# Window attention and two MLPs on one core: ScalarE's work for coming heads and GpSimd's low part of g put behind other instructions

## The chip, the core and the metric

The kernel runs on one core of one Trainium2 chip. The core has five engines that run side by side, each with a queue that it works through in order: TensorE (PE, with the weight load, PEld, shown apart), VectorE (DVE), ScalarE (ACT), GpSimd (POOL) and SyncE (SP), which issues the DMAs. The metric is the device time of one execution in microseconds (us), the median of three runs.

## The reference

Attention of 4 sequences of 576 tokens with 8 heads of 64 over a window of 128 tokens, with a slope per head, then two MLPs (512 to 2048 to 512) one after the other over all 2304 tokens.

```python
scores = scale * np.matmul(q, k.transpose(0, 1, 3, 2))
bias = slopes[:, None, None] * (-np.abs(rel).astype(np.float32))[None, :, :]
mask = (rel >= 0) & (rel < window)
scores = np.where(mask, scores + bias[None], -1000000000.0)
attn = np.exp(scores - np.max(scores, axis=-1, keepdims=True))
attn = attn / (np.sum(attn, axis=-1, keepdims=True) + 1e-09)
x = np.matmul(attn, v)           # to (tokens, heads * 64)
# first MLP
h = x @ w_in
g = np.where(h >= 1, h, np.where(h <= -1, 0.0, (h + 1) ** 2 / 4.0))
x = g @ w_out
# second MLP: h = x @ w_in2; g = h * clip(h + 3, 0, 6) / 6; out = g @ w_out2
```

## The kernel before

The tokens are cut into units of 64 to 256 queries. Each unit has 8 heads, so head 40 is the first of unit 5. A head's queries go in blocks of up to 128: heads 40 to 47, 56 to 63 and 88 to 95 have one block each, the other heads from 32 on have two. A step is one block of one head. Units 0 to 3 (heads 0 to 31) multiply in float32; from head 32 on every operand is split into a rounded high part and a low part (float32r), and only these heads' code is touched here.

The first MLP runs at the same time. It goes over blocks of tokens and 16 chunks f of its 2048 hidden columns. `Chunks.run` writes a chunk: 12 matmuls L659 into the bank h, then `between()`, in which an attention step (`tick`) may stand, then `flush`, the 12 matmuls L701 of the chunk two before (LAG = 2), then `after()`, where another step may stand. `activate` turns h into g: L688 on DVE, L689 on ACT, L690 on DVE, which frees the bank h, then g's high part on ACT (L152) and its low part on POOL (L159). From the wide blocks on there is one h bank, so that the next chunk's L659 waits for L690.

A step of a head from 32 on, `stage_a`: two matmuls L411 give the scores s from qs with kh and with kl. DVE masks and adds the slope (L438, L441, the smallest value by row), ACT takes exp with its sum (L445), DVE makes the reciprocal (L448, L449), POOL normalises p (L450). Three steps later, `stage_b`: PE transposes p (L470), ACT rounds the high part of it (L152, into tt, or into dist where a block has keys of the block before), DVE makes the low part (L483), and POOL cuts the two triangles (L488). Two steps after that, `stage_c`: L554 multiplies with vs into r. After a head's last block ACT and DVE add the halves of r to xf (L572), and after an odd head `to_x` casts xf to x, the MLP's input (L152 on ACT, L159 on DVE).

`prep(n)` casts a head's operands ahead: on ACT kh (L389) and the high part of qs (L390), on DVE kl (L391), on POOL the low part of qs (L393, with a memset L395 where a block is short), and for an even head vs (L152, L159). `tick` calls it right behind `stage_a` of a head's first block: for head n+1 where the heads have two blocks, and up to head n+2 where they have one.

```python
with self.behind():
    for x in late:
        self.to_x(*x)
    if i == 0:
        self.more_preps(n + 1 if u.whole or len(u.qbs) > 1 else n + 2)
```

The order within an engine is found by a scheduler while the program is built; SP's is as written. `tc.issue_after(ins)` binds it: what is written inside, on the engine of `ins`, stands behind `ins`. `behind()` opens it for the last L441 (`row`), L483 (`low`) and L572 (`sum`), all three on DVE. It holds for the casts and for `flush`.

Of the kernel before, what the change touches and what calls it, by code (L numbers as in the profile page):

```python
# [40 lines left out]
def tile_window_attention_two_mlps(  # L41
# [108 lines left out]
    def split_hi(eng, hi, x):  # L150
        if eng == "act":
            nc.scalar.copy(hi, x)  # L152
        elif eng == "pool":
            nc.gpsimd.tensor_scalar(out=hi, in0=x, scalar1=1.0, scalar2=1.0, op0=ALU.mult, op1=ALU.mult)
        else:
            engines[eng].tensor_copy(hi, x)

    def split_lo(eng, lo, x, hi):
        engines[eng].tensor_tensor(out=lo, in0=x, in1=hi.bitcast(F32), op=ALU.subtract)  # L159
# [110 lines left out]
    class Attention:  # L270
        def __init__(self, raw, proc, work, xs):
            self.raw, self.proc, self.work, self.xs = raw, proc, work, xs
            self.n_load = self.n_prep = self.t = 0
            self.row, self.low, self.sum, self.late = None, None, None, []
            self.k_owners, self.v_owners = [], []
# [138 lines left out]
        def stage_a(self, n, i):  # L414
# [20 lines left out]
            if not u.whole and a >= P:  # L435
# [8 lines left out]
                scalar=3.0e38, op0=ALU.add, op1=ALU.min, accum_out=sm[:, 0:1])  # L444
            nc.scalar.activation(out=pt[:, :nk], in_=pt[:, :nk], func=AF.Exp, bias=sm[:, 0:1],  # L445
                                 scale=-1.0, accum_out=None if u.whole else sm[:, 1:2])
            if not u.whole:
# [6 lines left out]
        def stage_b(self, n, i):  # L454
# [26 lines left out]
            hi, lo = both[:, 0], both[:, 1]  # L481
            split_hi(HI["th"], hi, src)
            self.low = nc.vector.tensor_tensor(out=lo, in0=src, in1=hi.bitcast(F32), op=ALU.subtract)  # L483
            if has_prev:


                for s, sign in ((0, -1), (1, 1)):
                    nc.gpsimd.affine_select(out=u.tt[:, :, s0 + s, :m], in_=both, compare_op=ALU.is_ge, fill=0.0,  # L488
                                            base=-1 + s, pattern=[[0, 2], [sign, m]], channel_multiplier=-sign)
# [140 lines left out]
        def behind(self):  # L630


            stack = ExitStack()
            for op in (self.row, self.low, self.sum):
                if op:
                    stack.enter_context(tc.issue_after(op.ins))
            return stack


    class Mlp:  # L640
        tags = ("h0", "h1")
        g_lo = "g"
# [29 lines left out]
    class Mlp1(Mlp):  # L672
        acc_tags = ("acc0", "acc1", "h1", "t2")
        lag = LAG

        def accs(self, n):
# [7 lines left out]
        def activate(self, ps, n):  # L684


            r, g = self.tiles()
            nc.vector.tensor_scalar(out=r[:, :n], in0=ps[:, :n], scalar1=-1.0, scalar2=1.0, op0=ALU.max, op1=ALU.min)  # L688
            self.square = nc.scalar.activation(out=r[:, :n], in_=r[:, :n], func=AF.Square, bias=0.5, scale=0.5)  # L689
            self.larger = nc.vector.tensor_tensor(out=r[:, :n], in0=ps[:, :n], in1=r[:, :n], op=ALU.max)  # L690
            split_hi(HI["g"], g[:, 0, :n], r[:, :n])
            split_lo(LO[self.g_lo], g[:, 1, :n], r[:, :n], g[:, 0, :n])
            return g
# [35 lines left out]
    class Mlp2(Mlp):  # L729
# [4 lines left out]
        def between(self):  # L734
            pass
# [43 lines left out]
    class Chunks:  # L779
# [22 lines left out]
        def run(self, mlp, blk, f, part, x, between, after, behind=ExitStack):  # L802
            self.pend.append((mlp, blk, f, part, mlp.first(x, f, mlp.blocks[blk][1])))
            between()
            with behind():
                self.flush(mlp.lag)
            after()
# [28 lines left out]
    def run_block(mlp1, j, part, hook):  # L836
        for f in part:
            chunks.run(mlp1, j, f, part, j, lambda: hook(f, 0), lambda: hook(f, 1), att.behind)

    with ExitStack() as actx:  # L840
# [507 lines left out]
```

## Time and profile before

| | us |
|---|---|
| median of 3 runs (lowest, highest) | 946.19 (946.13, 946.76) |
| profiled execution | 946.02 |
| its span, first to last instruction | 944.3 |
| TensorE busy in it | 928.5 (98%) |
| VectorE, ScalarE, GpSimd busy | 659.4, 535.6, 306.8 |

The split heads' attention and the first MLP run between about 165 and 480 us. The second MLP follows and is not touched. The granted TensorE clock is 1.000 of full speed over the span. A row of the timeline gives the start, the duration, the engine, the line and the operation as out<-in; consecutive instructions of one line stand in one row with their count (x12), and what is in brackets at its end is the engine's idle time before it and the instruction that ended it.

### The profile page before, as it was taken

How to read it: one execution, taken by the hardware profiler on the slowest of the kernel's cores; microseconds unless marked ns; L12 is line 12 of the kernel's file. 1: busy time of each engine (PE TensorE's matmuls, PEld its weight loads, DVE VectorE, ACT ScalarE, POOL GpSimd, SP SyncE). 2: the span in 40 equal slices, each digit the busy share in tenths (PEclk: the TensorE clock that was granted, in tenths of full speed). 3: DMA queues.
4: the chain of work that ended last, by engine and by line, in shares of the span. 5: the costliest groups of instructions: out<-in, count | busy, mean ns of one | idle time of the engine just before them, and what ended most of it. 6: DMA issues, size and time to landing. Idle time of an engine off the chain costs nothing.

```text
span 944.3 us, 17237 instructions
## 1 busy us (share of the span) xinstructions
PE 928.5 (98%) x5683; PEld 875.5 (93%) x5683; DVE 659.4 (70%) x1750; ACT 535.6 (57%) x1349; POOL 306.8 (32%) x575
## 2 busy tenths in 40 slices
PE   8899999999999999999999999999999999999998
PEld 6799999999999999999999999999999888898987
DVE  6998975786677677767656899958557777644443
ACT  6998854676667566666635786535333334423233
POOL 3243845787668676777710000000000000000000
PEclk9999999999999999999999999999999999999999
DMA  8858322232222212322017771004264654543431
GB/s 256 240 178 264 111 89 88 68 86 67 73 64 72 79 46 62 89 75 62 1 55 270 266 237 55 1 23 167 81 210 170 232 174 146 169 124 114 123 112 67
DMA packets 95337, 114.90 MB, mean 122 GB/s; under 512 B 8848, under 2 KB 73616, under 8 KB 95248
## 3 DMA queue, kind: packets, MB, share of 16 engines
q1 hardware_dynamic: 95248, 113.80, 38.3%
q8 instruction: 45, 0.74, 0.3%
q14 instruction: 44, 0.36, 0.1%
HBM read 88.60 MB, written 25.17 MB: 120 GB/s over the span
## 4 chain that ended last, share of the span: by engine, by line
PE 89%; DVE 5%; ACT 2%; DMA 2%; issue 1%; POOL 1%; SPq 0%; ACTq 0%; DVEq 0%; POOLq 0%
PE h L659 26%; PE acc L760 21%; PE acc L701 18%; PE y L1249 7%; PE x L1249 5%; PE s L411 4%; PE r L554 3%; PE t L470 2%; PE r L506 2%; DMA rawa<-w_in 1%; DVE r L688 1%; DVE kl L391 1%; DVE r L690 1%; DVE x L159 1%; DMA kw<-kT 1%
## 5 line engine op out<-in xcount | busy, mean ns | idle before, releaser
L659 PE MATMUL h<-x,wa 128*128 128x384 f32 (+1 forms) x1344 | 231.0, 317 | 1.4 <-DVE r L690 0.9
L701 PE MATMUL acc<-g,wa 128*128 128x384 f32 (+1 forms) x1344 | 227.4, 315 | 0.4 <-POOL g L159 0.4
L760 PE MATMUL acc<-wb,g 128*128 128x512 f32 x861 | 222.2, 393 | 0.0
L659 PEld LDWEIGHTS h<-x,wa 128*128 128x128 f32 x1344 | 206.8, 189 | 4.3 <-DVE r L690 3.4
L701 PEld LDWEIGHTS acc<-g,wa 128*128 128x128 f32 x1344 | 206.3, 189 | 0.7 <-POOL g L159 0.6
L760 PEld LDWEIGHTS acc<-wb,g 128*128 128x128 f32 x861 | 159.4, 188 | 24.9
L152 ACT CAST g<-r 128x384 fp32r<-128x384 f32 (+1 forms) x208 | 101.6, 489 | 71.4 <-DVE r L1196 37.6
L159 POOL TENSOR_TENSOR g<-r,g 128x256 fp32r<-128x256 f32 (+1 forms) x96 | 92.5, 964 | 67.7 <-ACT g L152 54.8
L689 ACT ACTIVATE r<-r 128x384 f32<-128x384 f32 (+1 forms) x112 | 53.5, 479 | 81.3 <-DVE r L688 81.0
L159 DVE TENSOR_TENSOR g<-r,g 128x384 fp32r<-128x384 f32 x112 | 62.4, 557 | 41.9 <-ACT g L152 41.6
L688 DVE TENSOR_SCALAR r<-h 128x384 f32<-128x384 f32 (+1 forms) x112 | 55.4, 495 | 44.0 <-PE h L659 37.3
L488 POOL TENSOR_SCALAR_AFFINE_SELECT tt<-dist 128x256 fp32r<-128x256 f32 (+1 forms) x176 | 76.9, 458 | 13.9 <-DVE dist L483 13.8
L690 DVE TENSOR_TENSOR r<-h,r 128x384 f32<-128x384 f32 (+1 forms) x112 | 55.8, 499 | 30.3 <-ACT r L689 28.4
L659 PE MATMUL h<-x,wb 128*128 128x384 f32 x384 | 72.5, 336 | 0.0
L659 PEld LDWEIGHTS h<-x,wb 128*128 128x128 f32 x384 | 68.2, 188 | 2.6
L445 ACT ACTIVATE p<-p,sm 128x128 f32<-128x128 f32 (+2 forms) x134 | 57.3, 430 | 20.9 <-DVE sm L441 20.5
L1194 ACT ACTIVATE r<-u 128x384 f32<-128x384 f32 x32 | 16.9, 527 | 56.2 <-DVE u L1258 56.2
L554 PEld LDWEIGHTS r<-tt,vs 128*128 128x128 f32 x304 | 44.7, 189 | 3.2 <-issue 1.4
L393 POOL TENSOR_TENSOR qs<-qr,qs 128x256 fp32r<-128x256 f32 (+2 forms) x64 | 39.4, 616 | 24.9 <-ACT qs L390 13.3
L554 PE MATMUL r<-tt,vs 128*128 128x128 f32 (+3 forms) x304 | 44.3, 262 | 1.4 <-POOL tt L488 0.9
L470 PE MATMUL t<-ident,p 128*128 128x128 f32 x134 | 38.4, 288 | 0.5 <-ACT tt L152 0.5
L1249 PE MATMUL y<-wb,w 128*128 128x384 f32 x192 | 38.7, 336 | 0.0
(161 smaller groups left out, 1554.6 us busy)
## 6 DMA issues: line engine op xcount, KB each, us to landing
w<-wd SPq DMA_DIRECT2D x88, 256.0 KB, 2.7
rawa<-w_in SPq DMA_DIRECT2D x16, 512.0 KB, 5.3
rawa<-w_out SPq DMA_DIRECT2D x16, 512.0 KB, 5.4
rawb<-w_in SPq DMA_DIRECT2D x16, 512.0 KB, 3.8
rawb<-w_out SPq DMA_DIRECT2D x16, 512.0 KB, 4.7
wd<-sum SPq DMA_DIRECT2D x32, 256.0 KB, 2.1
wd<-wb SPq DMA_DIRECT2D x24, 256.0 KB, 2.8
out<-o SPq DMA_DIRECT2D x17, 256.0 KB, 2.3
```

Source lines behind the costliest of these rows:

```text
L152: nc.scalar.copy(hi, x)
L159: engines[eng].tensor_tensor(out=lo, in0=x, in1=hi.bitcast(F32), op=ALU.subtract)
L445: nc.scalar.activation(out=pt[:, :nk], in_=pt[:, :nk], func=AF.Exp, bias=sm[:, 0:1], scale=-1.0, accum_out=None if u.whole else sm[:, 1:2])
L470: nc.tensor.transpose(ps[:, 1, :], pt[:, P:] if u.whole and has_prev else pt[:, :P], ident)
L488: nc.gpsimd.affine_select(out=u.tt[:, :, s0 + s, :m], in_=both, compare_op=ALU.is_ge, fill=0.0, base=-1 + s, pattern=[[0, 2], [sign, m]], ...
L554: nc.tensor.matmul(u.r[:, qo:qo + nq], u.vs[:, j, c, :, :].rearrange("p a d -> p (a d)"), u.tt[:, part].rearrange("p s q -> p (s q)")[:, s ...
L659: nc.tensor.matmul(ps[:, :n], self.W.w_in(a, c, f), self.x_chunk(x, b, c, n), start=(k == 0), stop=(k == 3 * KC - 1))
L688: nc.vector.tensor_scalar(out=r[:, :n], in0=ps[:, :n], scalar1=-1.0, scalar2=1.0, op0=ALU.max, op1=ALU.min)
L690: self.larger = nc.vector.tensor_tensor(out=r[:, :n], in0=ps[:, :n], in1=r[:, :n], op=ALU.max)
L701: nc.tensor.matmul(acc[i][:, o * n:(o + 1) * n], self.W.w_out(a, f)[:, e * P:(e + 1) * P], g[:, b, :n], start=(first and k == 0 and o == 0 ...
L760: nc.tensor.matmul(acc[t][:, :DM], g[:, b, tg * P:(tg + 1) * P], self.W.w_out(a, f), start=(first and k == 0), stop=(last and k == 2))
L1249: nc.tensor.matmul(ps[:, :N2], w[:, a, c * P:(c + 1) * P], self.x.operand(k, c, b), start=(start and n == 0), stop=(n == 5), skip_group_ch ...
```

## The change

`behind()` binds two more instructions: the last exp (L445) and the last rounded transpose (L152 in `stage_b`) of the heads from 32 on. Both are on ACT, so ACT's part of `prep`, of `to_x` and of `flush` stands behind them. The low part of g is no longer written in `activate` but in `Chunks.run`, after `between()`, and stands behind the last triangle (L488) on POOL. This holds in the blocks that `run_block` writes, once there has been a triangle. Computation and instruction counts stay the same.

```diff
--- before.py
+++ after.py
@@ -149,7 +149,7 @@
 
     def split_hi(eng, hi, x):
         if eng == "act":
-            nc.scalar.copy(hi, x)
+            return nc.scalar.copy(hi, x)
         elif eng == "pool":
             nc.gpsimd.tensor_scalar(out=hi, in0=x, scalar1=1.0, scalar2=1.0, op0=ALU.mult, op1=ALU.mult)
         else:
@@ -271,7 +271,7 @@
         def __init__(self, raw, proc, work, xs):
             self.raw, self.proc, self.work, self.xs = raw, proc, work, xs
             self.n_load = self.n_prep = self.t = 0
-            self.row, self.low, self.sum, self.late = None, None, None, []
+            self.row, self.low, self.sum, self.exp, self.high, self.tri, self.late = None, None, None, None, None, None, []
             self.k_owners, self.v_owners = [], []
 
             self.vts = [raw.tile([P, KCH, 2 * D + 2], F32, tag="vr", name=f"vr{i}", bufs=3) for i in range(3)]
@@ -442,8 +442,10 @@
                 out=pt[:, :nk], in0=ps[:, :nk], in1=table,
                 scale=-scale if u.whole else -slopes[u.h],
                 scalar=3.0e38, op0=ALU.add, op1=ALU.min, accum_out=sm[:, 0:1])
-            nc.scalar.activation(out=pt[:, :nk], in_=pt[:, :nk], func=AF.Exp, bias=sm[:, 0:1],
-                                 scale=-1.0, accum_out=None if u.whole else sm[:, 1:2])
+            exp = nc.scalar.activation(out=pt[:, :nk], in_=pt[:, :nk], func=AF.Exp, bias=sm[:, 0:1],
+                                       scale=-1.0, accum_out=None if u.whole else sm[:, 1:2])
+            if not u.whole:
+                self.exp = exp
             if not u.whole:
                 nc.vector.tensor_scalar(out=sm[:, 2:3], in0=sm[:, 1:2], scalar1=EPS, scalar2=None, op0=ALU.add)
                 nc.vector.reciprocal(sm[:, 3:4], sm[:, 2:3])
@@ -479,13 +481,13 @@
             else:
                 both = u.tt[:, :, s0 + 1, :m]
             hi, lo = both[:, 0], both[:, 1]
-            split_hi(HI["th"], hi, src)
+            self.high = split_hi(HI["th"], hi, src)
             self.low = nc.vector.tensor_tensor(out=lo, in0=src, in1=hi.bitcast(F32), op=ALU.subtract)
             if has_prev:
 
 
                 for s, sign in ((0, -1), (1, 1)):
-                    nc.gpsimd.affine_select(out=u.tt[:, :, s0 + s, :m], in_=both, compare_op=ALU.is_ge, fill=0.0,
+                    self.tri = nc.gpsimd.affine_select(out=u.tt[:, :, s0 + s, :m], in_=both, compare_op=ALU.is_ge, fill=0.0,
                                             base=-1 + s, pattern=[[0, 2], [sign, m]], channel_multiplier=-sign)
 
         def stage_c_whole(self, n, i):
@@ -631,13 +633,14 @@
 
 
             stack = ExitStack()
-            for op in (self.row, self.low, self.sum):
+            for op in (self.row, self.low, self.sum, self.exp, self.high):
                 if op:
                     stack.enter_context(tc.issue_after(op.ins))
             return stack
 
 
     class Mlp:
+        late_low = False
         tags = ("h0", "h1")
         g_lo = "g"
         opool = cpool
@@ -672,6 +675,7 @@
     class Mlp1(Mlp):
         acc_tags = ("acc0", "acc1", "h1", "t2")
         lag = LAG
+        late_low = False
 
         def accs(self, n):
             return [psum.tile([P, BANK], F32, tag=self.acc_tags[i], name=f"acc{i}")
@@ -689,7 +693,9 @@
             self.square = nc.scalar.activation(out=r[:, :n], in_=r[:, :n], func=AF.Square, bias=0.5, scale=0.5)
             self.larger = nc.vector.tensor_tensor(out=r[:, :n], in0=ps[:, :n], in1=r[:, :n], op=ALU.max)
             split_hi(HI["g"], g[:, 0, :n], r[:, :n])
-            split_lo(LO[self.g_lo], g[:, 1, :n], r[:, :n], g[:, 0, :n])
+            self.low = lambda: split_lo(LO[self.g_lo], g[:, 1, :n], r[:, :n], g[:, 0, :n])
+            if not self.late_low:
+                self.low()
             return g
 
         def second(self, acc, g, f, n, first, last):
@@ -801,8 +807,12 @@
 
         def run(self, mlp, blk, f, part, x, between, after, behind=ExitStack):
             self.pend.append((mlp, blk, f, part, mlp.first(x, f, mlp.blocks[blk][1])))
+            late = mlp.late_low
             between()
             with behind():
+                if late:
+                    with tc.issue_after(att.tri.ins):
+                        mlp.low()
                 self.flush(mlp.lag)
             after()
 
@@ -835,7 +845,9 @@
 
     def run_block(mlp1, j, part, hook):
         for f in part:
+            mlp1.late_low = att.tri is not None
             chunks.run(mlp1, j, f, part, j, lambda: hook(f, 0), lambda: hook(f, 1), att.behind)
+        mlp1.late_low = False
 
     with ExitStack() as actx:
         mlp1 = Mlp1(W1, blocks1, rpool, gpool)
```

In the program after, lines 441 to 449 of before keep or shift by up to 2 (L448 to L450, L449 to L451, L450 to L452, L488 to L490, L554 to L556, L572 to L574), and L659, L688, L689, L690, L701 become L662, L692, L693, L694, L707. The names carry a head's number: kh89 is kh of head 89, sm88_0 belongs to block 0 of head 88, t86_1 is the transpose of block 1 of head 86; dist_97 is the buffer of a block with triangles; p0, p1, p2 are buffers of p.

ACT around head 89, before:

```order
L152 CAST dist_97<-t86_0_6853 128x128
L689 ACTIVATE r_6842<-r_6842 128x384
L389 ACTIVATE kh89_6905<-kr88_6612 128x256
L390 ACTIVATE qs89_6907<-qr88_6613,minus_odd_72 128x128
L152 CAST g_6843<-r_6842 128x384
L445 ACTIVATE dist_97,sm87_1_6862<-dist_97,sm87_1_6862 128x128
L152 CAST vs88_6824<-vr2_104 128x2x64 x2
L152 COPY xf84_6791<-r85_6849 64x256
L152 CAST dist_97<-t86_1_6887 128x128
L389 ACTIVATE kh90_6912<-kr90_6801 128x256
L445 ACTIVATE p0_113,sm88_0_6896<-p0_113,sm88_0_6896 128x128
L152 CAST x_78<-xf84_6791 128x256
```

ACT at the same place, after:

```order
L152 CAST dist_97<-t86_1_6887 128x128
L445 ACTIVATE p0_113,sm88_0_6896<-p0_113,sm88_0_6896 128x128
L389 ACTIVATE kh89_6905<-kr88_6611 128x256
L152 CAST x_78<-xf84_6791 128x256
L390 ACTIVATE qs89_6907<-qr88_6612,minus_odd_72 128x128
L389 ACTIVATE kh90_6912<-kr90_6801 128x256
L390 ACTIVATE qs90_6914<-qr90_6802,minus_odd_72 128x128
L152 CAST dist_97<-t87_0_6954 128x128
L693 ACTIVATE r_6944<-r_6944 128x384
```

kh89 and qs89 stood a step earlier, ahead of the exp of head 87's second block; now they stand behind the exp of head 88's only block, with x between them, and kh90 is behind that exp too.

POOL around head 57, before:

```order
L393 TENSOR_TENSOR qs57_4213<-qr56_3934,qs57_4213 128x128
L450 TENSOR_SCALAR dist_97<-dist_97,sm55_1_4168 128x128
L159 TENSOR_TENSOR g_4153<-r_4152,g_4153 128x384
L159 TENSOR_TENSOR vs56_4134<-vr1_103,vs56_4134 128x2x64 x2
L488 AFFINE_SELECT tt54_4160<-dist_97 128x2x128 x2
L450 TENSOR_SCALAR p0_113<-p0_113,sm56_0_4202 128x128
L393 TENSOR_TENSOR qs58_4220<-qr58_4113,qs58_4220 128x128
L393 TENSOR_TENSOR qs59_4275<-qr58_4113,qs59_4275 128x128
```

POOL at the same place, after:

```order
L159 TENSOR_TENSOR vs56_4134<-vr1_103,vs56_4134 128x2x64 x2
L490 AFFINE_SELECT tt54_4159<-dist_97 128x2x128 x2
L452 TENSOR_SCALAR p0_113<-p0_113,sm56_0_4202 128x128
L393 TENSOR_TENSOR qs57_4213<-qr56_3933,qs57_4213 128x128
L393 TENSOR_TENSOR qs58_4220<-qr58_4113,qs58_4220 128x128
L159 TENSOR_TENSOR g_4251<-r_4250,g_4251 128x384
L452 TENSOR_SCALAR p1_114<-p1_114,sm57_0_4265 128x128
```

The low part of qs57 stood five rows ahead of the normalisation with sm56_0; now it stands right behind it.

PE around head 57, before:

```order
L470 MATMUL t55_0_4259<-ident_70,p2_115 128x128
L411 MATMUL s57_0_4263<-kh57_4211,qs57_4213 128x256
L411 MATMUL s57_0_4263<-kl57_4212,qs57_4213 128x256
L701 MATMUL acc0_3883<-g_4064,wa5_739 128x384 x3
L701 MATMUL acc1_3884<-g_4064,wa5_739 128x384 x3
```

PE at the same place, after:

```order
L472 MATMUL t55_0_4258<-ident_70,p2_115 128x128
L707 MATMUL acc0_3883<-g_4064,wa5_739 128x384 x2
L411 MATMUL s57_0_4262<-kh57_4211,qs57_4213 128x256
L411 MATMUL s57_0_4262<-kl57_4212,qs57_4213 128x256
L707 MATMUL acc0_3883<-g_4064,wa5_739 128x384
```

Two matmuls L701 (L707 after) went ahead of the scores of head 57. At head 41 four went ahead in the same way, and two more between its two score matmuls; elsewhere PE's order is the same but for one L554.

## Rows read from the trace of the kernel before

**Rows 1.** page part 1: busy time, share of the span and instructions of TensorE

```profile
PE 928.5 (98%) x5683; PEld 875.5 (93%) x5683; DVE 659.4 (70%) x1750; ACT 535.6 (57%) x1349; POOL 306.8 (32%) x575
```

**Rows 2.** sums of four stretches, 165 to 480 us: length, busy us of each engine

```profile
sum 315.00, PE 311.95 PEld 305.65 DVE 224.38 ACT 206.23 POOL 227.68; mean PE 77.99 PEld 76.41 DVE 56.10 ACT 51.56 POOL 56.92
```

**Rows 3.** page part 5: line, operation, count, busy us, mean ns, idle before it and releaser

```profile
L659 PE MATMUL h<-x,wa 128*128 128x384 f32 (+1 forms) x1344 | 231.0, 317 | 1.4 <-DVE r L690 0.9
...
L554 PE MATMUL r<-tt,vs 128*128 128x128 f32 (+3 forms) x304 | 44.3, 262 | 1.4 <-POOL tt L488 0.9
```

**Rows 4.** timeline 438 to 442.2 us: start, duration, engine, line, operation

```profile
438.11 0.36 PE L411 MATMUL s<-kh,qs 128*128 128x256 f32 x1
...
439.35 0.42 ACT L389 ACTIVATE kh<-kr 128x256 fp32r<-128x256 f32 x1
...
440.12 0.95 POOL L488 TENSOR_SCALAR_AFFINE_SELECT tt<-dist 128x256 fp32r<-128x256 f32 x2 [0.42 <-DVE dist L483]
...
440.35 0.40 ACT L390 ACTIVATE qs<-qr,minus_odd 128x128 fp32r<-128x128 f32 x1
...
440.77 0.36 PE L411 MATMUL s<-kh,qs 128*128 128x256 f32 x1
440.80 0.55 DVE L159 TENSOR_TENSOR x<-xf,x 128x256 fp32r<-128x256 f32 x1
...
441.06 0.79 POOL L450 TENSOR_SCALAR p<-p,sm 128x128 f32<-128x128 f32 x1
...
441.81 0.46 POOL L393 TENSOR_TENSOR qs<-qr,qs 128x128 fp32r<-128x128 f32 x1
```

**Rows 5.** timeline 262.4 to 268.6 us

```profile
264.93 1.19 POOL L488 TENSOR_SCALAR_AFFINE_SELECT tt<-dist 128x256 fp32r<-128x256 f32 x2 [0.26 <-DVE dist L483]
...
265.21 0.36 PE L411 MATMUL s<-kh,qs 128*128 128x256 f32 x1
...
265.59 2.24 PE L701 MATMUL acc<-g,wa 128*128 128x384 f32 x12
...
266.10 0.53 POOL L450 TENSOR_SCALAR p<-p,sm 128x128 f32<-128x128 f32 x1
...
266.60 0.88 POOL L393 TENSOR_TENSOR qs<-qr,qs 128x128 fp32r<-128x128 f32 x2
```

**Rows 6.** timeline 186.8 to 192.8 us

```profile
187.90 0.46 POOL L393 TENSOR_TENSOR qs<-qr,qs 128x128 fp32r<-128x128 f32 x1 [1.31 <-DVE sm L441]
...
190.11 1.01 POOL L159 TENSOR_TENSOR vs<-vr,vs 128x128 fp32r<-128x128 f32 x2
...
190.34 0.36 PE L411 MATMUL s<-kh,qs 128*128 128x256 f32 x1
190.41 0.42 DVE L391 SCALAR_TENSOR_TENSOR kl<-kr,kh 128x256 fp32r<-128x256 f32 x1
...
190.88 0.39 PE L411 MATMUL s<-kl,qs 128*128 128x256 f32 x1 [0.17 <-DVE kl L391]
...
191.07 1.14 POOL L488 TENSOR_SCALAR_AFFINE_SELECT tt<-dist 128x256 fp32r<-128x256 f32 x2
191.10 1.60 PE L701 MATMUL acc<-g,wa 128*128 128x256 f32 x12
...
192.20 0.37 POOL L450 TENSOR_SCALAR p<-p,sm 128x128 f32<-128x128 f32 x1
```

**Rows 7.** timeline 316.3 to 319.7 us

```profile
318.37 0.37 POOL L450 TENSOR_SCALAR p<-p,sm 128x128 f32<-128x128 f32 x1
...
318.79 0.59 POOL L393 TENSOR_TENSOR qs<-qr,qs 128x192 fp32r<-128x192 f32 x1
...
318.96 0.36 PE L411 MATMUL s<-kh,qs 128*128 128x256 f32 x1
```

**Rows 8.** timeline 397.4 to 401 us

```profile
397.52 0.88 DVE L391 SCALAR_TENSOR_TENSOR kl<-kr,kh 128x384 fp32r<-128x384 f32 x1
...
398.87 0.53 DVE L688 TENSOR_SCALAR r<-h 128x384 f32<-128x384 f32 x1
```

## Prediction, made before the changed kernel ran

> **What bounds the kernel now.** I read the busy table first: TensorE (PE) is busy for 928.5 of 944.3 us, at full granted clock [rows 1]. So the change can only matter by what PE waits for, and in the 315 us in which the changed code runs (165 to 480 us) PE is busy for 311.95 us. The difference, 3.05 us, bounds what any reordering of the other engines can win there [rows 2]. Next I read the groups of PE's instructions for what ended their idle time: the first MLP matmuls (L659) sat idle for 1.4 us, 0.9 of it until L690 on VectorE (DVE) had freed the only h bank, and the L554 matmuls for 1.4 us, 0.9 of it until GpSimd's (POOL's) triangles L488 [rows 3]. Those are the two waits that the two halves of the change could remove. Last I read the timeline around each instruction that the change moves, and asked how long ahead of its reader it had been done.
>
> **What the change moves.** No instruction is added or taken away. From head 32 on, ScalarE's (ACT's) casts for coming heads (kh L389, qs L390), its x and o copies, and with them the DVE and POOL instructions that read them, stand behind the latest exp and the latest rounded transpose. What counts is the lead of a head's casts over its own scores (L411). In a unit with two blocks, head n+1 is cast in the step of head n's first block, two steps ahead. In a unit with one block, head n+2 is cast in the step of head n, again two steps ahead. Only where a one-block unit follows a two-block unit, at heads 40, 56 and 88, does one step cast two heads, and the first of them (41, 57, 89) has its scores one step later. Before, the scheduler moved these casts up past the exp. The new condition forbids it: the order of ACT now has exp of head 88, then kh89, x, qs89, and POOL's has triangles, normalisation L450, then qs89's low part L393. At these three places a chain from one head's scores to the next head's scores arises that was not there. Behind the casts on ACT stand the next rounded transpose, whose reader L554 comes two steps later and which I cost at nothing, and the MLP's L689, whose delay is held in the bounds of the DVE term. SP's order is unchanged; the loads (L351) that wait for a cast to free a buffer serve heads that are two steps off, and if that cover fails the price is within the bound of the other heads.
>
> **Head 89.** Its scores start at 440.77, the scores of head 88 at 438.11 [rows 4]: the step lasts 2.66 us. On ACT little is lost, since kh90 (L389 at 439.35, 0.42) leaves its place ahead of exp and kh89 takes one behind it; qs89 would then leave ACT where qs90 did, at 440.35 + 0.40 = 440.75 [rows 4]. POOL is later: the two triangles run from 440.12 for 0.95, to 441.07, then comes L450, which took 0.79 there, though 0.37 elsewhere [rows 6, 7], then L393 with 0.46. So qs89 is done at 441.06 + 0.37 + 0.46 = 441.89 at the earliest and at 442.31 with the longer L450. From a cast's end to the matmul that waits for it pass 0.05 (kl41 ends at 190.41 + 0.42 = 190.83, its matmul starts at 190.88 [rows 6]). PE waits 1.17 to 1.59; I take 1.3, since kl89 and x on DVE lie a little differently beside L450 now.
>
> **Head 57.** The triangles end at 264.93 + 1.19 = 266.12, L450 at 266.10 + 0.53 = 266.63, and L393, 0.88 for two, so 0.44 for one, at 267.07 [rows 5]. The new PE order puts two L701 matmuls ahead of these scores; twelve take 2.24, two 0.37, so PE arrives at 265.21 + 0.37 = 265.58 [rows 5]. The wait is 1.54, or 1.38 with an L450 of 0.37. I take 1.4.
>
> **Head 41.** vs ends at 190.11 + 1.01 = 191.12, the triangles at 191.07 + 1.14 = 192.21, L450 at 192.57, L393 of 0.46 at 193.03 [rows 6]. From this up to 0.46 goes off, since qs41 (L393 at 187.90) no longer stands in this queue earlier on. Four L701 matmuls are put ahead, at 1.60 / 12 = 0.13 each, so PE arrives at 190.34 + 0.53 = 190.87 [rows 6]. The wait is 1.75 to 2.21; PE's own wait there before, 0.17 for kl41, goes away in it. Net 1.58 to 2.04, and I take 1.6. The three places: 1.3 + 1.4 + 1.6 = **4.3 us** (4.1 to 5.2). The moved L701 matmuls cover what they can and are counted.
>
> **The other heads** have two steps, and most casts stay in time. Head 68 is of the tight ones: L450 ends at 318.37 + 0.37 = 318.74, L393 with 0.59 behind it at 319.33, its scores start at 318.96, so 0.42 with the 0.05 [rows 7]. I count six such heads by the lead of their exp; from 0 to 2.5 us, I take **0.6**, because the triangles ahead are mostly done before the scores there.
>
> **DVE.** kl (L391) is moved from the time in which DVE waits for exp to behind L449. At 397.52 it takes 0.88, and L688, which opens the chain to the h bank, starts at 398.87 [rows 8]; in two chunks it now stands straight ahead of L688. That costs 0 to 1.8. In the three unit changes one kl fewer stands ahead of it, and L690 is moved up past L441 in several steps. I take **0.4** net, with -0.6 to 1.8 as ends.
>
> **What is won.** At most both waits of rows 3, 0.9 + 0.9 = 1.8, and all idle time, 3.05, if exp and the rounded transposes come sooner everywhere. For L554 the longest wait ends when the low part of g no longer stands ahead of the triangles; but POOL then does g and a normalisation ahead of a later head's qs, so the next scores are late instead. Waits for the h bank that lie within a few us behind heads 41, 57 and 89 are swallowed by the new ones. I take **-1.3** (0 to -3.05). The low part of g itself costs nothing: its reader, L701, comes two chunks later. If that cover were gone, each pair of triangles ahead of it (0.95 to 1.19 [rows 4, 5]) would be on the path.
>
> **Sum.** 4.3 + 0.6 + 0.4 - 1.3 = 4.0 us. The profiled execution took 946.02 us, 1.7 us more than its span, and 0.17 below the median of 946.19. 946.02 + 4.0 = **950.0 us**; this case by itself goes from 948.1, the least loss that can be measured, to 952.2, with the places at 5.2 and nothing won.
>
> **A rule of the skill.** L450 took 0.79 us at 441.06, beside an x cast of DVE from 440.80 to 441.35, against 0.37 in other steps [rows 4, 6, 7]. The Trainium skill, page "Trainium Architecture — The Big Picture", section "What this means for kernel authors", says that on the engine side of SBUF only VectorE and GpSimd contend, for a port pair that is locked by one of them, not shared. The row agrees with it, though it shows no lock. By the rule the sum becomes that of the first rival below; by L450's 0.37 at head 41, with DVE's x cast just over, it stays. It speaks against this change, since kl is moved to where POOL works on the chain above.
>
> **Rivals.** *Stretched GpSimd chain.* kl and x on DVE stand beside L450 and L393 at the three places, and both instructions stretch as L450 did, by 0.79 - 0.37 = 0.42 each: 3 x 0.84 = 2.5 more, **952.4**. For it: L450's 0.79. Against: it took 0.53 at head 57 and 0.37 at head 41 [rows 5, 6]. The skill's rule above would make it so. Chance 0.09. *Even.* The places cost their lower ends, 4.1, nothing else is lost, and all 3.05 of idle time are won: 946.02 + 1.1, about **947.0**. For it: exp and the transposes do move up on ACT in nearly every step. Against: a good part of the idle time has other releasers. Chance 0.16. *Gain.* The triangles at the three places are done by the time the casts come, because ACT's rounded transpose is no longer behind casts and g's low part is behind the triangles. Then only ACT's end counts: 440.75 + 0.46 + 0.05 = 441.26 against 440.77, 0.49 at each, 1.5 in all, against 3.05 won: **944.5**, from 943.8 to 945.2. It decides from the point at which qs of 41, 57 and 89 is done within 0.5 us of PE's arrival. Against it: the transpose at head 89 stood ahead of exp before too, and its triangles started at 440.12 without g in the way. Chance 0.20, half of it below 944.3. *No effect*, that the scheduler gave the old order, is excluded by the order itself.
>
> **Chances.** My forecast 0.55, stretched 0.09, even 0.16, gain 0.20. 0.2%, about what a measurement of this kernel tells from no change, is 1.9 us: faster (below 944.3) 0.10, the same (to 948.1) 0.26, slower 0.64. The range leaves out the lower three quarters of the gain, 0.15, and half of the stretched case: 944.8 to 952.4.
>
> **What the next profile would show.** Right: the matmuls L411 of heads 41, 57 and 89 wait, each 1.2 to 2.2 us, and what ends the wait is POOL's L393; PE's busy time stays at 928.5 and its idle time grows by about 4 us, nearly all of it there. L554's wait for the triangles is gone, and a wait for a later head's qs stands near it. Wrong: if these three waits stay under 0.6 us, or end with ACT's cast or with kl, the main term fails. If they are there and the time is still the same, the gain was undersized: the waits of L659 for L690 would be gone in many chunks. If the time is over 952.4, kl or GpSimd's longer chain holds up more heads than the six.

## The result and the profile after

The changed kernel takes 957.79 us (median of 4 runs, 956.99 to 958.33), the kernel before 946.48 us (4 runs, 946.13 to 947.95). The ratio is 1.0114, with a 95% interval of 1.0099 to 1.013: 11.3 us slower. The direction was forecast, the size was not: 4.0 us were expected, and the time lies above the range (944.8 to 952.4 us).

The page of the changed kernel (busy table, and the groups of part 5: line, count, busy us, mean ns, idle time before it and what ended most of it):

```profile
PE 932.4 (98%) x5683; PEld 876.4 (92%) x5683; DVE 660.3 (69%) x1750; ACT 537.2 (56%) x1349; POOL 302.5 (32%) x575
...
L662 PE MATMUL h<-x,wa 128*128 128x384 f32 (+1 forms) x1344 | 230.9, 317 | 2.0 <-DVE r L694 1.5
...
L490 POOL TENSOR_SCALAR_AFFINE_SELECT tt<-dist 128x256 fp32r<-128x256 f32 (+1 forms) x176 | 66.1, 399 | 52.4 <-DVE dist L485 50.5
...
L411 PE MATMUL s<-kh,qs 128*128 128x256 f32 (+1 forms) x104 | 36.4, 350 | 5.4 <-POOL qs L393 4.6
```

TensorE's busy time rose by 3.9 us over [rows 1], and the scores L411 now sit idle for 5.4 us, 4.6 of it until GpSimd's L393. L662 (L659 before) waits 1.5 us for the h bank where it waited 0.9 [rows 3]. The row of the triangles, L490, shows something that the prediction left out: GpSimd now stands idle for 52.4 us in front of them, and did so for 13.9 us before.

The stretch of the changed code, which in the kernel before takes 315.00 us from 165 to 480 us, here lasts from 166.3 to 490.9 us (length, then busy us and instruction count of each engine):

```profile
166.30:490.90 324.60, 314.46 (x2095) 305.68 (x2095) 224.85 (x849) 208.93 (x695) 225.66 (x461) 1.00 0.22 62
```

It has the work of the 2096 matmuls of before (one more or less at the edges) and is 324.60 - 315.00 = 9.6 us longer. PE is idle in it for 10.14 us instead of 3.05 [rows 2], and its busy time is 2.51 us more. The weight loads (PEld) tell the same more plainly: they are busy for 305.68 us, as before (305.65), so they stand idle for 9.6 us more, which is the whole lengthening. The rest of the longer span is 1.4 us, and 1.3 of it lie ahead of the changed code: 1.0 us within the first 8 us and 0.3 near 64 us. The same score matmul is issued here

```profile
7.44 0.53 PE L411 MATMUL s<-kw,qw 128*128 128x256 f32 x1
```

and in the kernel before here:

```profile
6.40 0.60 PE L411 MATMUL s<-kw,qw 128*128 128x256 f32 x2
```

Nothing is changed at that place, and in the profiles of all ten experiments it lies 0.1 to 0.9 us later than in the kernel before too. The matmuls L125 that stand between the scores there took 0.42 us each up to 7.22 us in the changed kernel, and 0.27 us from 5.41 us on in the kernel before, so that PE only came to its faster pace later. The profile of before was lucky there, and I leave that part out.

The waits of the weight loads from 160 to 500 us, by line, tile and releaser (us in all, times, longest):

```profile
PEld s L411 <- POOL qs L393: 6.1, 6, 1.7
PEld h L662 <- DVE r L694: 3.7, 7, 0.9
...
PEld t L472 <- DVE tt L485: 1.4, 1, 1.4
PEld r L556 <- POOL vs L159: 1.2, 1, 1.2
```

These add up in many small places. The three places that the prediction named come first. Timeline of the changed kernel at head 41 (start, duration, engine, line, operation, idle time before it):

```profile
191.38 0.83 POOL L159 TENSOR_TENSOR vs<-vr,vs 128x128 fp32r<-128x128 f32 x2
...
192.17 0.76 POOL L490 TENSOR_SCALAR_AFFINE_SELECT tt<-dist 128x256 fp32r<-128x256 f32 x2
...
192.92 0.78 POOL L452 TENSOR_SCALAR p<-p,sm 128x128 f32<-128x128 f32 x1
...
193.67 1.02 POOL L393 TENSOR_TENSOR qs<-qr,qs 128x128 fp32r<-128x128 f32 x2
...
194.33 0.39 PE L411 MATMUL s<-kh,qs 128*128 128x256 f32 x1 [1.47 <-POOL qs L393]
```

at head 57:

```profile
271.39 0.53 POOL L452 TENSOR_SCALAR p<-p,sm 128x128 f32<-128x128 f32 x1
...
271.88 1.05 POOL L393 TENSOR_TENSOR qs<-qr,qs 128x128 fp32r<-128x128 f32 x2
...
272.39 0.39 PE L411 MATMUL s<-kh,qs 128*128 128x256 f32 x1 [0.96 <-POOL qs L393]
```

and at head 89:

```profile
450.23 0.53 POOL L452 TENSOR_SCALAR p<-p,sm 128x128 f32<-128x128 f32 x1
...
450.73 1.05 POOL L393 TENSOR_TENSOR qs<-qr,qs 128x128 fp32r<-128x128 f32 x2
...
451.23 0.39 PE L411 MATMUL s<-kh,qs 128*128 128x256 f32 x1 [1.05 <-POOL qs L393]
```

The order is the one that was argued: triangles, normalisation L452, L393, and then the scores. PE is idle for 1.47, 0.96 and 1.05 us, 3.48 in all; forecast were 1.6, 1.4 and 1.3. Two of the tight heads come next, head 37 and head 68:

```profile
173.10 0.39 PE L411 MATMUL s<-kh,qs 128*128 128x256 f32 x1 [0.72 <-POOL qs L393]
```

```profile
327.06 0.39 PE L411 MATMUL s<-kh,qs 128*128 128x256 f32 x1 [0.45 <-POOL qs L393]
```

### The profile page after: what moved, and what is told of

It is laid out like the page before. It is cut to its first block, busy times and chain, and to the rows that moved or that the text cites. A ratio compares the mean times of both kernels' runs of the same rounds, so it can differ in the third digit from the quotient of the medians.

```text
span 955.3 us, 17219 instructions
## 1 busy us (share of the span) xinstructions
PE 932.4 (98%) x5683; PEld 876.4 (92%) x5683; DVE 660.3 (69%) x1750; ACT 537.2 (56%) x1349; POOL 302.5 (32%) x575
## 4 chain that ended last, share of the span: by engine, by line
PE 79%; DVE 8%; ACT 4%; DMA 3%; issue 3%; POOL 2%; SPq 0%; ACTq 0%; POOLq 0%; DVEq 0%
PE h L662 23%; PE acc L766 21%; PE acc L707 15%; PE y L1261 7%; PE x L1261 5%; PE s L411 3%; PE r L556 2%; PE t L472 1%; PE r L508 1%; DVE r L694 1%; DVE r L692 1%; DMA rawa<-w_out 1%; ACT p L445 1%; ACT r L693 1%; DVE x L159 1%
## 5 line engine op out<-in xcount | busy, mean ns | idle before, releaser
L662 PE MATMUL h<-x,wa 128*128 128x384 f32 (+1 forms) x1344 | 230.9, 317 | 2.0 <-DVE r L694 1.5
L707 PE MATMUL acc<-g,wa 128*128 128x384 f32 (+1 forms) x1344 | 228.1, 315 | 0.4 <-POOL g L159 0.4
L662 PEld LDWEIGHTS h<-x,wa 128*128 128x128 f32 x1344 | 206.7, 189 | 4.8 <-DVE r L694 3.7
L707 PEld LDWEIGHTS acc<-g,wa 128*128 128x128 f32 x1344 | 206.5, 189 | 0.7 <-POOL g L159 0.6
L152 ACT CAST g<-r 128x384 fp32r<-128x384 f32 (+1 forms) x208 | 101.5, 488 | 83.7 <-DVE r L1208 37.6
L159 POOL TENSOR_TENSOR g<-r,g 128x256 fp32r<-128x256 f32 (+1 forms) x96 | 90.5, 944 | 52.2 <-ACT g L152 39.7
L693 ACT ACTIVATE r<-r 128x384 f32<-128x384 f32 (+1 forms) x112 | 53.4, 478 | 70.7 <-DVE r L692 69.1
L490 POOL TENSOR_SCALAR_AFFINE_SELECT tt<-dist 128x256 fp32r<-128x256 f32 (+1 forms) x176 | 66.1, 399 | 52.4 <-DVE dist L485 50.5
L692 DVE TENSOR_SCALAR r<-h 128x384 f32<-128x384 f32 (+1 forms) x112 | 55.4, 494 | 36.6 <-PE h L662 33.2
L694 DVE TENSOR_TENSOR r<-h,r 128x384 f32<-128x384 f32 (+1 forms) x112 | 55.7, 498 | 28.7 <-ACT r L693 27.6
L445 ACT ACTIVATE p<-p,sm 128x128 f32<-128x128 f32 (+2 forms) x134 | 57.2, 429 | 29.6 <-DVE sm L441 29.1
L662 PE MATMUL h<-x,wb 128*128 128x384 f32 x384 | 72.5, 336 | 0.0
L662 PEld LDWEIGHTS h<-x,wb 128*128 128x128 f32 x384 | 68.2, 188 | 2.6
L556 PEld LDWEIGHTS r<-tt,vs 128*128 128x128 f32 x304 | 44.4, 189 | 4.9 <-issue 2.6
L556 PE MATMUL r<-tt,vs 128*128 128x128 f32 (+3 forms) x304 | 44.8, 263 | 1.7 <-POOL vs L159 1.0
L450 DVE TENSOR_SCALAR sm<-sm 128x1 f32<-128x1 f32 x104 | 15.9, 153 | 41.7 <-ACT p L445 30.3
L452 POOL TENSOR_SCALAR p<-p,sm 128x128 f32<-128x128 f32 x78 | 39.2, 502 | 12.8 <-DVE sm L451 5.9
L411 PE MATMUL s<-kh,qs 128*128 128x256 f32 (+1 forms) x104 | 36.4, 350 | 5.4 <-POOL qs L393 4.6
```

The source lines that it names most:

```text
L152: return nc.scalar.copy(hi, x)
L411: nc.tensor.matmul(ps[:, :nk], q[:, qo:qo + P], k[:, ko:ko + nk], start=(w == 0), stop=(w == len(parts) - 1))
L445: exp = nc.scalar.activation(out=pt[:, :nk], in_=pt[:, :nk], func=AF.Exp, bias=sm[:, 0:1], scale=-1.0, accum_out=None if u.whole else sm[: ...
L490: self.tri = nc.gpsimd.affine_select(out=u.tt[:, :, s0 + s, :m], in_=both, compare_op=ALU.is_ge, fill=0.0, base=-1 + s, pattern=[[0, 2], [ ...
L556: nc.tensor.matmul(u.r[:, qo:qo + nq], u.vs[:, j, c, :, :].rearrange("p a d -> p (a d)"), u.tt[:, part].rearrange("p s q -> p (s q)")[:, s ...
L662: nc.tensor.matmul(ps[:, :n], self.W.w_in(a, c, f), self.x_chunk(x, b, c, n), start=(k == 0), stop=(k == 3 * KC - 1))
```

## Experiments

Theory A: the loss is that ScalarE's casts for coming heads stand behind exp. Theory B: the loss is the low part of g behind the triangles. Theory C came after the first four results: neither alone, but the two together, by way of GpSimd's queue. Each run was compared with runs of the kernel before on the same chip (946.7 to 946.9 us).

| kernel | casts bound to | low part of g | us (median) | ratio to before, 95% interval |
|---|---|---|---|---|
| changed kernel | exp, transpose | late | 957.79 | 1.0114 (1.0099 to 1.013) |
| e1 | exp | on time | 952.63 | 1.0062 (1.0047 to 1.0077) |
| e2 | as before | late | 945.21 | 0.9983 (0.9974 to 0.9992) |
| e3 | as before, x and flush bound | late | 945.58 | 0.9988 (0.9978 to 0.9997) |
| e4 | exp, transpose; 41, 57, 89 early | late | 955.35 | 1.0084 (1.0067 to 1.01) |
| e5 | transpose | on time | 951.04 | 1.004 (1.0024 to 1.0056) |
| e6 | exp, transpose | behind earlier triangles | 953.23 | 1.0068 (1.0052 to 1.0084) |
| e7 | exp, transpose; 41, 57, 89 early | on time | 951.09 | 1.0046 (1.003 to 1.0062) |
| e8 | as before; 41, 57, 89 early | late | 943.71 | 0.9966 (0.9953 to 0.998) |
| e9 | as before; 41, 57, 89 early | on time | 945.34 | 0.9983 (0.9973 to 0.9992) |
| e10 | as before; 41, 57, 89 early | behind earlier triangles | 945.33 | 0.9981 (0.9971 to 0.999) |

**e1: the binding without the late low part.**

```diff
-            for op in (self.row, self.low, self.sum, self.exp, self.high):
+            for op in (self.row, self.low, self.sum, self.exp):
...
-            mlp1.late_low = att.tri is not None
```

> Only exp is bound in behind(); g's low part is written where it was before. Theory A (the loss is ScalarE's casts standing behind exp): the loss stays, 953 to 957, and the scores of heads 41, 57 and 89 wait 1.1 to 1.6 us each for L393, as in the changed kernel. Theory B (the loss comes from g's low part standing behind the triangles, which makes GpSimd late for vs, p and qs): the time falls back to 946 to 949. The order of the instructions is the same with exp alone as with exp and the rounded transpose, so this run is also both bindings without the late low part.

952.63 us, 5.8 above before and 5.2 below the changed kernel. Theory A accounts for about half of the loss, theory B is wrong as it stands. With exp bound, binding the rounded transpose as well gives the same program.

**e2: the late low part without the binding.**

```diff
-            for op in (self.row, self.low, self.sum, self.exp, self.high):
+            for op in (self.row, self.low, self.sum):
```

> Only g's low part stands behind the triangles; behind() binds what it did before. Theory A: the casts are ahead of exp again, the three waits at heads 41, 57 and 89 are gone, and the time is 945 to 948. Theory B: most of the 11 us stay, 952 to 957, with TensorE waits that end with vs (L159) and the normalisation on GpSimd.

945.21 us, 1.6 below before. So the late low part is a gain alone and a loss of 957.79 - 952.63 = 5.2 us on top of the binding. The two halves of the change are not additive: 5.8 - 1.6 = 4.2 would be their sum, 11.3 is what they cost.

**e3: only the casts are let go.**

```diff
+                with self.behind(False):
                     if i == 0:
                         self.more_preps(n + 1 if u.whole or len(u.qbs) > 1 else n + 2)
...
-        def behind(self):
+        def behind(self, all=True):
...
-            for op in (self.row, self.low, self.sum, self.exp, self.high):
+            for op in (self.row, self.low, self.sum) + ((self.exp, self.high) if all else ()):
```

> The changed kernel, but the casts for coming heads (kh, qs, vs and their low parts) are bound by the three instructions of before only; the casts to x and the flush stay bound by exp and the rounded transpose, and g's low part by the triangles. Theory A: all waits for L393 go, 946 to 949. Theory B: 952 to 957. If the casts to x and the flush behind exp were the loss, it would also stay above 952, with waits of another kind.

945.58 us. It differs from the changed kernel only in the casts for coming heads, and 12.2 us go with them. Against e2, the casts to x and the flush behind exp cost 0.4 us, which is within the width of the two intervals.

**e4: heads 41, 57 and 89 are cast one step earlier in the changed kernel.** (e7 does the same with the low part on time, e8 without the new bindings, e9 in the kernel before.)

```diff
                     if i == 0:
                         self.more_preps(n + 1 if u.whole or len(u.qbs) > 1 else n + 2)
+                    elif not u.whole and i == len(u.qbs) - 1 and n + 1 < len(heads) and len(heads[n + 1].qbs) == 1:
+                        self.more_preps(n + 2)
```

> The changed kernel, with heads 41, 57 and 89 cast one step earlier, in the last step of the two-block head before them; the bindings stay. Theory A in its first form: the three waits of 1.63, 1.12 and 1.29 us go and nothing else, so 957.8 - 4.0 = 953.8. If those waits only cover others that come up in their place: 956 or more. If the three places set off the later waits too: under 951.

955.35 us, 2.4 less than the changed kernel instead of 4.0. The three waits are gone from the trace; they count 3.48 us as PE's idle time and 4.18 as that of the weight loads. The single runs go from 953.16 to 956.14, and the profiled one, at 955.93, holds two losses that are not of this edit: a stretch at half the granted clock (last section) and a wait of 1.14 us of the first MLP's matmul (L664 in this program) near 532 us, in the tail block, that no other profile here has. The one run whose mean granted clock was 1.000 is the fastest, 953.16, and it is 3.8 and 5.2 us below the two runs of the changed kernel at 1.000 (956.99 and 958.33). So e4 is not a clean measure of the three places: by the medians 2.4 us came back, by that one run about the whole 4.0.

**e5: only the rounded transpose is bound.**

```diff
-            for op in (self.row, self.low, self.sum, self.exp, self.high):
+            for op in (self.row, self.low, self.sum, self.high):
...
-            mlp1.late_low = att.tri is not None
```

> Only the rounded transpose is bound in behind(), and g's low part is written as before. At heads 41, 57 and 89 the low part of qs still stands behind the normalisation, but kh goes ahead of exp again. Theory A with ScalarE's place as the cost: a good part of the 5.8 us of binding exp goes, 947 to 950. Theory A with GpSimd's place as the cost (L393 behind triangles and normalisation): the three waits stay, 951 to 953.

951.04 us, at the lower edge of what GpSimd's place would give. kh41, kh57 and kh89 stand ahead of exp again there, and the three score matmuls still wait, for 1.36, 1.47 and 1.05 us. At head 89:

```profile
444.46 0.41 ACT L390 ACTIVATE qs<-qr,minus_odd 128x128 fp32r<-128x128 f32 x1
...
445.67 1.05 POOL L393 TENSOR_TENSOR qs<-qr,qs 128x128 fp32r<-128x128 f32 x2
...
446.18 0.39 PE L411 MATMUL s<-kh,qs 128*128 128x256 f32 x1 [1.05 <-POOL qs L393]
```

ScalarE's cast of qs ends at 444.87, 0.80 us before GpSimd gets to L393. So what makes these three waits is L393's place behind the triangles and the normalisation, not the casts' place on ScalarE. The time decides less: the two runs at a mean granted clock of 1.000 took 948.97 and 949.42 us, in the range that was given for ScalarE's place, the three at 0.998 took 951.04 to 951.77. Against e1 1.6 us are gone by the medians, and nearly 3 at a clock of 1.000 (e1: 952.18); that part goes with the binding of exp, and I can't assign it to one place.

**e6: the low part of g behind the triangles of an earlier step.**

```diff
-            late = mlp.late_low
+            late, tri = mlp.late_low, att.tri
...
-                    with tc.issue_after(att.tri.ins):
+                    with tc.issue_after(tri.ins):
```

> The changed kernel, but g's low part stands behind the triangles that were written last before the step, not behind those of the step itself. Theory C (with the casts bound, g's low part behind the step's triangles costs 5 us more because GpSimd stands idle in front of the triangles and does g, the normalisation, qs and vs after them, too late): GpSimd's idle time ahead of the triangles falls from 52 us to under 20 and the time to that of the binding alone, 952 to 953.5. If the extra 5 us come from another cause (another order on VectorE or ScalarE), it stays above 956.

953.23 us: 4.6 of the 5.2 us are gone, as theory C expected. The triangles' rows of e1, of e2 and of this kernel, in that order (the idle time in front of them stands behind the second bar):

```profile
L490 POOL TENSOR_SCALAR_AFFINE_SELECT tt<-dist 128x256 fp32r<-128x256 f32 (+1 forms) x176 | 73.7, 440 | 12.5 <-DVE dist L485 11.2
```

```profile
L490 POOL TENSOR_SCALAR_AFFINE_SELECT tt<-dist 128x256 fp32r<-128x256 f32 (+1 forms) x176 | 75.0, 449 | 37.3 <-DVE dist L485 36.8
```

```profile
L490 POOL TENSOR_SCALAR_AFFINE_SELECT tt<-dist 128x256 fp32r<-128x256 f32 (+1 forms) x176 | 72.8, 436 | 14.0 <-DVE dist L485 12.8
```

The order of the instructions says more than the expectation asked. In the traces of e1, of e6 and of the changed kernel PE, DVE and ACT do their instructions in one and the same order from the first to the last; only GpSimd's differs (and the kernel before and e2 differ in GpSimd's order alone, too). So another order on VectorE or ScalarE is no cause of the 5.2 us. On GpSimd, all but about ten of e6's 575 instructions stand where e1 has them: e6 is close to e1 by its making, so its time confirms e1's and is no second measure.

GpSimd waits in front of the triangles for 12.5 us in e1, 37.3 in e2, 14.0 here, and 52.4 in the changed kernel. The wait by itself does no harm: e2 has 37.3 us of it and is the fastest of the four. It harms where the work that was put behind it is wanted soon. At vs of head 44, GpSimd and PE of the changed kernel:

```profile
208.22 0.76 POOL L490 TENSOR_SCALAR_AFFINE_SELECT tt<-dist 128x256 fp32r<-128x256 f32 x2 [1.09 <-DVE dist L485]
...
208.95 0.74 POOL L159 TENSOR_TENSOR g<-r,g 128x256 fp32r<-128x256 f32 x1
...
211.09 0.82 POOL L159 TENSOR_TENSOR vs<-vr,vs 128x128 fp32r<-128x128 f32 x2 [0.45 <-ACT vs L152]
...
211.97 0.63 PE L556 MATMUL r<-tt,vs 128*128 128x128 f32 x4 [1.00 <-POOL vs L159]
```

and of e1:

```profile
206.47 0.73 POOL L159 TENSOR_TENSOR g<-r,g 128x256 fp32r<-128x256 f32 x1 [0.71 <-DVE dist L485]
...
207.16 0.76 POOL L490 TENSOR_SCALAR_AFFINE_SELECT tt<-dist 128x256 fp32r<-128x256 f32 x2
...
209.28 0.83 POOL L159 TENSOR_TENSOR vs<-vr,vs 128x128 fp32r<-128x128 f32 x2 [0.39 <-ACT vs L152]
...
210.17 0.63 PE L556 MATMUL r<-tt,vs 128*128 128x128 f32 x4 [0.18 <-POOL vs L159]
```

In e1 the low part of g fills the time before the triangles. In the changed kernel GpSimd waits 1.09 us for the triangles' input, then makes the triangles, then g, and everything behind moves back: vs, cast late by ScalarE, is made from 211.09, and L556 waits 1.00 us for it, 0.18 in e1.

**e7: early casts with the binding, low part on time.** The edit of e4, with g's low part as in e1; exp and the rounded transpose are both bound, which gives the same program as exp alone.

> Exp and the rounded transpose are bound, g's low part is written as before, and heads 41, 57 and 89 are cast one step earlier. If the three waits of 1.49, 1.25 and 1.28 us are what the binding costs: 952.6 - 4.0 = 948.6. If they are replaced by others: 951 or more. If the rest of the binding gains: 947 or less.

951.09 us, 1.5 below e1 instead of 4.0. The two profiled runs, both at a granted clock of 1.000, are 2.1 us apart (950.07 and 952.18). The waits of the weight loads in e1:

```profile
PEld s L411 <- POOL qs L393: 5.8, 6, 1.6
PEld h L662 <- DVE r L694: 2.8, 5, 0.7
...
PEld r L556 <- POOL vs L159: 0.4, 1, 0.4
```

and in e7:

```profile
PEld h L664 <- DVE r L696: 3.8, 7, 0.7
PEld s L411 <- POOL qs L393: 1.6, 3, 0.7
...
PEld r L556 <- POOL vs L159: 0.8, 1, 0.8
```

The waits for L393 fall by 4.2 us, as expected. But the waits for the h bank rise by 1.0 and that for vs by 0.4. Behind heads 57 and 89 the weight loads of e7 wait 0.55 and 0.23 us for the h bank, where the kernel before waits too (0.55 and 0.37) and e1 does not: there the waits for L393 had covered them, since the other engines caught up while PE stood. That leaves 2.8 us, against 2.1 between the profiled runs; the rows don't show where the rest went.

**e8: late low part, early casts, no binding.** The edits of e2 and e4 together.

> g's low part late, no new binding in behind(), and heads 41, 57 and 89 cast one step earlier. Without the binding the casts are ahead of exp anyway, so the earlier cast should change little against the late low part alone: 944.5 to 945.5. If the wait of 0.33 us for kl41 and the h waits behind the unit changes go with it: 943.5 to 944.5. If the earlier casts stand in the way of the step before: 946 to 947.

943.71 us, 3.0 below before: the best of the versions, ahead of both the kernel before and the changed one.

**e9: the kernel before with the early casts.** The edit of e4 alone.

> The kernel before, with heads 41, 57 and 89 cast one step earlier and nothing else changed. If the gain of the late low part (1.6 us) and that of the earlier casts add up to the 3.0 us of both together: 945.2 against 946.7. If the earlier cast only helps where g's low part is late: 946.5. If it stands in the way of the step before: 947 or more.

945.34 us, 1.6 below before. Late low part 1.6, early casts 1.6, both 3.0: here the two edits do add up. At the unit changes of the kernel before the prediction had seen only the 0.17 us for kl41.

**e10: e8 with the low part of g behind earlier triangles.** The edits of e8 and e6 together.

> No new binding in behind(), heads 41, 57 and 89 cast one step earlier, and g's low part behind the triangles written last before the step. Theory C says that without the bound casts GpSimd can stand in front of the triangles at no cost, so this should not beat the version with the step's own triangles: 943.7 to 945.5. If standing there costs even then: under 943.2.

945.33 us, equal to e9: this place of g's low part wins nothing. It is also nearly e9's program: PE, DVE and ACT have the same order in both, and so have all but about 14 of GpSimd's 575 instructions. The waits of the weight loads behind the triangles, in e10, and the largest group of the same matmuls in e8:

```profile
PEld r L556 <- POOL tt L490: 1.1, 1, 1.1
```

```profile
PEld r L556 <- issue: 0.9, 3, 0.4
```

The wait of 1.1 us for the triangles (of which PE itself stood idle for 0.9 in the kernel before [rows 3]) is in e10 and not in e8. By its size it is two thirds of what the late low part is worth, and it goes only where the step's own triangles come first; the other third is not assigned.

## Why the prediction was wrong

**What bounds the kernel** was right: PE's idle time in one stretch grew from 3.05 to 10.14 us, and the other engines' busy times hardly changed. Two of its signs failed. PE's busy time did not stay at 928.5 us (932.4), and of the 7.1 us of idle time that came on top only 3.48 stand at the three places, not nearly all.

**The three unit changes** (4.3 us forecast) were right in place, releaser and size: 3.48 us of idle time, each with L393 as releaser. Net they are less. Taking them away won 1.5 us by the medians and 2.1 between the profiled runs (e7 against e1), since they swallow waits behind them. The prediction knew this and put it into the gain of -1.3.

**"The low part of g itself costs nothing: its reader, L701, comes two chunks later."** This is the step that failed. L707 doesn't wait for g, but GpSimd's queue does: what stands behind g (normalisation, low part of qs, vs) waits with it, behind triangles whose input comes late. I asked who reads g. What is queued behind it I asked at one place only (L554, where "POOL then does g and a normalisation ahead of a later head's qs"), and gave it no price, while I myself had moved qs into that very queue by the other half of the change. So the late low part stood in the sum as a gain, and on top of the binding it cost 5.2 us (changed kernel against e1, where only GpSimd's order differs; e6, with g further forward, has 4.6 of them back). The row to look at was GpSimd's idle time in front of the triangles, 13.9 us in the kernel before: the work ahead of them was what filled that time.

**The other heads** (0.6 forecast, 0 to 2.5): head 37 waits 0.72 and head 68 0.45, against 0.42 worked out for the latter. So the price of one was right for head 68. Of the six heads that were counted two have PE wait for L393, 1.17 us in all, and the waits at vs were not thought of. The last sign of being wrong, that GpSimd's longer chain holds up more heads than the six, named the right engine; it was not more heads that waited but vs, the transposes and the h bank as well.

**The gain** (-1.3): with the binding, none of it is seen. L659's waits for the h bank rose from 0.9 to 1.5 us. The wait of L554 for the triangles went, and at the same place the transpose L472 now waits 1.24 us for DVE's L485:

```profile
365.19 1.00 POOL L159 TENSOR_TENSOR g<-r,g 128x384 fp32r<-128x384 f32 x1
365.23 1.17 DVE L159 TENSOR_TENSOR x<-xf,x 128x192 fp32r<-128x192 f32 x1
...
366.59 0.28 DVE L485 TENSOR_TENSOR tt<-t,tt 128x128 fp32r<-128x128 f32 x1
...
366.93 0.33 PE L472 MATMUL t<-ident,dist 128*128 128x128 f32 x1 [1.24 <-DVE tt L485]
```

Here g's low part has moved beside DVE's x cast. The cast takes 1.17 us and ends 0.21 us after g's 365.19 + 1.00 = 366.19. In e6, with g earlier against x:

```profile
361.55 1.00 POOL L159 TENSOR_TENSOR g<-r,g 128x384 fp32r<-128x384 f32 x1 [0.35 <-ACT g L152]
...
362.16 0.60 DVE L159 TENSOR_TENSOR x<-xf,x 128x192 fp32r<-128x192 f32 x1
```

it takes 0.60, and again ends 0.21 after g (361.55 + 1.00 = 362.55; 362.16 + 0.60 = 362.76). So it seems held until g has ended, whenever it began. The other casts of the changed kernel bear it out. Eight of its x casts begin while a low part of g runs, 0.04 to 0.46 us after it, and end behind it by the same time for their width: 0.15 us at 128x128 (three), 0.21 to 0.22 at 128x192 (four), 0.28 at 128x256 (one). One of them:

```profile
314.22 1.02 POOL L159 TENSOR_TENSOR g<-r,g 128x384 fp32r<-128x384 f32 x1
...
314.68 0.71 DVE L159 TENSOR_TENSOR x<-xf,x 128x128 fp32r<-128x128 f32 x1
```

This is the rule of the Trainium skill, page "Trainium Architecture — The Big Picture", section "What this means for kernel authors", that the port pair of VectorE and GpSimd is locked by one of them; the rows agree with a lock. The prediction used it for a rival at the three places, and there it did not decide: L452 took 0.78, 0.53 and 0.53 us, 1.84 in all, and L450 at the same places 0.37, 0.53 and 0.79, 1.69 in all [rows 4 to 6]. The prediction's case against the rule, the 0.37 at head 41 "with DVE's x cast just over", was no test of it: that cast ran from 190.82 for 0.58 us and was over 0.80 us before L450 began at 192.20.

**DVE** (0.4) can't be told apart from the rest by these runs.

**The rivals.** "Stretched" had the right direction and the wrong mechanism. "Even" and "gain" are what the late low part does without the binding (e2, e3): the gain was there, 1.6 us, and the binding took it away. Of the 11.3 us, the runs assign 5.8 to the bound casts (e1) and 5.2 to the late low part on top of them, all of it by GpSimd's order, and 4.6 of it gone when g moves forward (e6). The rows show two ways in which it costs, vs made late (1.00 us at head 44) and the x cast held by g (1.24 us at L472); how the 5.2 us divide between such places is not shown. How the timed 11.3 divide from the profiled 9.6 in the stretch is left open; the start and the granted clock (below) can both be in it.

## What to carry to other kernels

When an instruction is put behind another one on an in-order engine, price the queue behind it, not its own reader: whatever already stands there waits for the same input. Two such bindings that meet in one queue must be priced together, for here one alone won 1.6 us, the other alone cost 5.8, and both cost 11.3. And a wait that one removes may have been covering others: in e7 4.0 us of waits gave back 1.5 us by the medians and 2.1 between the profiled runs.

## What the runs showed of the hardware

TensorE's granted clock can fall to half after a wait of 1 to 2 us, and a wait at the same place may leave it alone. e6, us by us around head 41 (stretch, length, busy us of PE, PEld, DVE, ACT, POOL, then granted clock):

```profile
191.00:192.00 1.00, 0.07 (x1) 0.00 (x0) 1.00 (x3) 0.96 (x4) 1.00 (x2) 1.00 0.00 0
192.00:193.00 1.00, 0.37 (x3) 0.37 (x4) 0.01 (x1) 0.00 (x0) 0.99 (x3) 1.00 0.00 0
...
194.00:195.00 1.00, 1.00 (x7) 1.00 (x6) 0.45 (x4) 0.92 (x4) 0.68 (x2) 0.50 0.52 151
```

PE was busy for 0.07 and 0.37 us in two us, then runs at 0.50, its 1.2 GHz level, with 7 matmuls in 1 us. In the changed kernel PE waits at the same place, from 192.86 to 194.33, and the clock stays, with 11 matmuls in 1 us:

```profile
193.00:194.00 1.00, 0.00 (x0) 0.00 (x0) 0.97 (x3) 0.75 (x4) 1.00 (x2) 1.00 0.00 0
...
195.00:196.00 1.00, 1.00 (x11) 1.00 (x10) 0.89 (x4) 0.23 (x1) 0.00 (x0) 1.00 0.57 159
```

e4 and e5 show such a stretch from about 364.5 and 362 us on, behind waits of PE near head 75 (1.24 and 0.23 us in e4, 1.04 and 0.33 in e5). So a wait on PE can cost more than its length, in some executions. The single runs fit this: e7 took 950.07 and 950.30 us in the two runs whose mean granted clock was 1.000, and 951.88 and 952.09 in the two at 0.998; e5 took 948.97 and 949.42 at 1.000, and 951.04 to 951.77 in the three at 0.998. In the changed kernel the clock does not part the runs (956.99 and 958.33 at 1.000, 957.70 and 957.88 at 0.998).
